# Another written order for the first eleven stretches of an attention kernel

## The chip, the cores and the metric

The kernel runs on one core of one Trainium2 chip. The metric is the device time of one execution in microseconds (us); lower is better. Five engines work side by side, each in the order of its own instruction stream: TensorE (PE; its weight loads are the row PEld), VectorE (DVE), ScalarE (ACT), GpSimd (POOL) and SyncE (SP), which here issues most of the DMAs. They meet by semaphores only.

## What is computed

From the reference, cut to what matters (bfloat16; S = Sq = 2048 rows, D = 640, 32 heads of 192, a window of W = 512 keys; w_gate, w_up: 640 x 1536):

```python
xn = _layernorm(A_x)
# attention without a mask, over the last 512 keys of the cache
q = (xn @ wq).reshape(B, Sq, Hq, Dh).transpose(0, 2, 1, 3)
scores = jnp.einsum("bhqd,bhkd->bhqk", q, k) * (Dh ** -0.5)
p = _softmax(scores, axis=-1)
s = jnp.einsum("bhqk,bhkd->bhqd", p, v) ... @ wo
# two rows of xn, those with the largest xn @ w_r, get a gated FFN's output added
b = _B_ref(xn, w_r, w_gate, w_up, w_down)
out = A_x + s * _silu(b)
```

## The kernel before

**Tiles.** The 2048 rows are 16 tiles of 128. A *step* i is one of (group g of four heads, block t5 of four tiles, pair pr of two heads), in that order; it has four *units*, one for each tile, n = 4 i + u. A unit is 128 rows by two heads. Units are put into *stretches*: S.0 and S.1 have two units each, all others three; there are 86 (0 to 85). All engines follow one written list of *tokens*: the function first (from L654 on) turns a token into instructions, and each engine gets its own in the order of the list. No scheduler changes that order (manual_schedule). The list of stretches 0 to 10 is the string FIRST; 11 to 84 are written by a function (stretch), and the last by another string.

**Tokens**, with unit n, head hh, step i:

- x.t5.lo.hi loads tiles lo to hi of block t5; k.p.hh, v.p, wq.p, wo.g.pr load keys, values and weights of a pair or group. An "a" at the end puts the load on ScalarE's queue instead of SP's.
- Statistics of a row tile: bn.n.c is half of one on VectorE (the second half also aggregates). as.n makes all of one tile's on ScalarE: two passes over 128x640 with a sum each (L235, L236), and a small step on GpSimd. sq, rc and pw make the reciprocal root: by ScalarE and VectorE, or by four GpSimd instructions for two or four tiles. sx and ex load tables of ScalarE's functions.
- ap.n.e writes the normalized tile xn on the engine e (v VectorE, a ScalarE, g GpSimd). turn.n.e turns it on TensorE and copies it out; xT.lo.hi turns two tiles by a DMA on SP. kt.q.e and kT.p do the same for keys. z.1 is one matmul on a tile of zeros, whose result nobody reads.
- q.i.c(.lo.hi) is one third (128 of the 384 columns) of a step's projection: five matmuls of 512 columns, or of 256 where lo.hi names half of the block. qe.i.c.e copies it, scaled, to SBUF.
- S.j: all scores of stretch j, two matmuls a head (contraction 128, L317, and 64, L324). M.n.hh: the negated row max (VectorE, L332). E.n.hh: exp with its row sum (ScalarE, L339). P.n: the unit's exps are turned by a DMA on SP (L344). O.n: eight matmuls with the values (L358). R.j: reciprocals of the sums. Oe.n.e: the output, divided, to SBUF. T.j(.lo.hi): its turning by a DMA on SP (L379). W.w: the product of one row tile with wo for a group, two times six matmuls of 320 columns (L406). We.w.e adds or copies it to the accumulator.
- B.j.slot runs background steps filed for that stretch. The earliest is filed for stretch 12, so every B in FIRST is empty.

**Buffers that order the work around the change.** Results of TensorE lie in two pools in PSUM, used in turn:

```python
    ps_f = pool("ps_f", 2, space=bass.MemoryType.PSUM)
    ps_p = pool("ps_p", 6, space=bass.MemoryType.PSUM)
```

From ps_f come turn, q, and an O without letter; from ps_p come scores (two a unit, so all six in a stretch of three units), W (two), kt, and an O with g. A matmul that opens a result waits until the one that had this buffer before is read: scores by E, q by qe, O by Oe, W by We. Exps have four buffers (freed when P has landed), pT and oT six, o_sb and x_in two: the load of block 2 waits for the ap of all four tiles of block 0, that of block 3 for block 1.

Of the kernel before, what the change touches and what calls it, by code (L numbers as in the profile page):

```python
# [21 lines left out]
def kernel(ctx, tc, A_x, A_k_cache, A_v_cache, A_wq, A_wo, B_x, B_w_r, B_w_gate, B_w_up, B_w_down, out):  # L22
    nc = tc.nc
    P = 128
    _, S, D = A_x.shape
# [3 lines left out]
    W = min(4096, max(256, Sk // 4))  # L29
# [412 lines left out]
    M = {}  # L442
# [347 lines left out]
    for j in range(2, NST):  # L790
        due = sum(st_of[4 * i] <= j + 1 for i, _ in todo)
        k = max(due, 2) if j % 4 != 1 else max(due, 3)
# [3 lines left out]
        k = 2 if len(ready) >= 2 and len(q_in[j]) <= 2 and (done + 1) <= 1.5 * (j - 4) else 1  # L796
        k = {NST - 4: 1, NST - 3: 1, NST - 2: 3, NST - 1: 2}.get(j, k)
# [69 lines left out]

    for token in FIRST:
# [43 lines left out]
```

## Time and profile before

| | us |
|---|---|
| median of 3 runs | 795.02 (794.94 to 795.55) |
| the profiled execution, its own time | 795.82 |
| its span, first to last instruction | 794.0 |
| TensorE busy | 783.4 |
| VectorE busy | 624.6 |
| ScalarE busy | 477.1 |
| GpSimd busy | 179.0 |

Times in views of the profile count from the span's start. A row of a timeline gives start, duration, engine, line, operation, output <- input, count, and in brackets the engine's idle time before it and who ended that. Consecutive instructions overlap at their ends, so the price of one in a series is the distance of starts. Section 2 of the page cuts the span in 40 slices and gives each engine's busy tenths; PEclk there is the clock granted to TensorE.

### The profile page before, as it was taken

To read this page: it belongs to the slowest core of one execution; us is meant where nothing else is said; L and a number is where in the kernel's file an instruction comes from. 1 tells how busy PE (TensorE), PEld (TensorE's weight loads), DVE (VectorE), ACT (ScalarE), POOL (GpSimd) and SP (SyncE) were. 2 spreads that over 40 slices of the span, in tenths; PEclk is the share of its full clock that TensorE was granted. 3 is DMA by queue.
4 is the path that set the end of the run, shared out by engine and by line. 5 is a ranking of instruction groups with operands and counts; after the bars stand their busy time and mean duration, and the time that the engine had idled before them with its cause. 6 is when DMAs were issued, how large, how long until landed. Compare 5 with 4: busy or idle time off the path is not lost. (4 is left out here: it accounts for less than half of the span.)

```text
span 794.0 us, 15678 instructions
## 1 busy us (share of the span) xinstructions
PE 783.4 (99%) x5758; PEld 481.9 (61%) x5759; DVE 624.6 (79%) x1247; ACT 477.1 (60%) x1285; POOL 179.0 (23%) x197
## 2 busy tenths in 40 slices
PE   8999999999999999999999999999999999999998
PEld 4456666656666566666566665666566666556666
DVE  7975677989787777777787777777788988777786
ACT  7856666557655656655566455566666865565651
POOL 3130000000010000000000599970000000165966
PEclk9999999999999999999999999999999999999999
DMA  9999998799989999799997999879998899998996
GB/s 255 194 198 204 197 212 152 138 179 192 194 134 207 201 192 218 136 220 192 202 217 150 170 170 199 169 136 179 200 159 149 134 192 190 184 195 151 181 163 141
DMA packets 453869, 143.80 MB, mean 181 GB/s; under 512 B 422446, under 2 KB 453424, under 8 KB 453792
## 3 DMA queue, kind: packets, MB, share of 16 engines
q1 hardware_dynamic: 452336, 140.39, 95.1%
q0 software_dynamic: 736, 1.84, 0.9%
q8 instruction: 45, 0.74, 0.4%
q10 hardware_dynamic: 720, 0.57, 0.3%
q14 instruction: 32, 0.26, 0.1%
HBM read 39.98 MB, written 2.62 MB: 54 GB/s over the span
## 5 line engine op out<-in xcount | busy, mean ns | idle before, releaser
L339 ACT ACTIVATE pexp<-sc,nm 128x512 bf16<-128x512 f32 x512 | 348.4, 697 | 266.0 <-issue 231.8
L332 DVE TENSOR_REDUCE nm<-sc 128x1 f32<-128x512 f32 x512 | 315.5, 683 | 77.1 <-PE sc L324 76.9
L303 PE MATMUL q_ps<-xnT,wq_p 128*128 128x512 bf16 (+1 forms) x980 | 225.9, 375 | 1.4 <-ACT o_sb L371 0.6
L406 PE MATMUL w_ps<-wo_g,oT 128*128 128x320 bf16 x1542 | 222.9, 298 | 0.0
L406 PEld LDWEIGHTS <-oT 128*128 128x128 bf16 x1542 | 150.3, 98 | 69.5
L358 PE MATMUL o_ps<-v_sb,pT 128*128 128x192 bf16 x2048 | 185.9, 246 | 2.3 <-DMA pT<-pexp 2.2
L358 PEld LDWEIGHTS <-pT 128*128 128x128 bf16 x2048 | 170.9, 98 | 18.6 <-DMA pT<-pexp 5.4
L373 DVE TENSOR_TENSOR o_sb<-o_ps,lsum 128x384 bf16<-128x384 f32 x244 | 134.6, 556 | 40.3 <-PE o_ps L358 22.2
L303 PEld LDWEIGHTS <-wq_p 128*128 128x128 bf16 x980 | 89.3, 98 | 124.4 <-issue 35.8
L317 PE MATMUL sc<-kT,qT 128*128 128x512 bf16 x512 | 125.2, 379 | 0.1
L420 DVE TENSOR_TENSOR s_acc<-s_acc,w_ps 128x320 f32<-128x320 f32 x192 | 92.6, 484 | 30.6 <-PE w_ps L406 30.6
L339 ACT ACTIVATION_READ_ACCUMULATOR pexp<-sc,nm 128x1 f32 x512 | 109.8, 215 | 0.0
L295 ACT ACTIVATE qT<-q_ps 128x512 bf16<-128x512 f32 (+1 forms) x179 | 99.3, 608 | 5.2 <-PE q_ps L303 5.1
L317 PEld LDWEIGHTS <-qT 128*128 128x128 bf16 x512 | 48.5, 98 | 41.8 <-issue 1.2
L324 PE MATMUL sc<-kT,qT 64*128 64x512 bf16 x512 | 70.2, 380 | 0.0
L324 PEld LDWEIGHTS <-qT 64*128 64x128 bf16 x512 | 18.0, 94 | 46.8 <-issue 35.8
L650 POOL TENSOR_TENSOR s_acc<-s_acc,xn 128x640 f32<-128x640 f32 x16 | 22.9, 1433 | 102.3 <-DVE s_acc L420 102.3
L629 POOL TENSOR_TENSOR xn<-xn,yh 128x640 bf16<-128x640 bf16 x32 | 44.6, 1394 | 2.7
L619 POOL DMA_DIRECT2D y_d<-y_sb x4 | 2.2, 551 | 181.2 <-DVE y_sb L616 181.2
L496 POOL DMA_DIRECT2D c_d<-cand x1 | 0.5, 544 | 163.7 <-DVE cand L494 163.7
L651 POOL TENSOR_TENSOR s_acc<-s_acc,x_fin 128x640 f32<-128x640 f32 x16 | 22.4, 1398 | 61.6 <-DVE lsum L348 54.5
L628 POOL TENSOR_SCALAR yh<-y_bc,oh 128x640 bf16<-128x640 bf16 x32 | 25.6, 799 | 6.0 <-DMA y_bc<-y_d 4.4
(109 smaller groups left out, 229.9 us busy)
## 6 DMA issues: line engine op xcount, KB each, us to landing
wq_p<-in_A_wq_dram SPq DMA_DIRECT2D x16, 480.0 KB, 4.7
wo_g<-in_A_wo_dram SPq DMA_DIRECT2D x16, 480.0 KB, 4.3
k_raw<-in_A_k_cache_dram SPq DMA_DIRECT2D x32, 192.0 KB, 3.4
v_sb<-in_A_v_cache_dram SPq DMA_DIRECT2D x16, 384.0 KB, 4.3
pT<-pexp SPq DMA_TRANSPOSE x256, 3.6
x_fin<-in_A_x_dram SPq DMA_DIRECT2D x16, 160.0 KB, 2.9
wgu<-in_B_w_gate_dram SPq DMA_DIRECT2D x15, 128.0 KB, 2.9
wgu<-in_B_w_up_dram SPq DMA_DIRECT2D x15, 128.0 KB, 3.7
```

Source lines behind the costliest of these rows:

```text
L295: nc.scalar.activation(out=out, in_=in_, func=ACT.Copy, scale=scale)
L303: nc.tensor.matmul(q_ps, lhsT=wq_of[g * PAIRS + pr][:, dc, c * P:(c + 1) * P], rhs=xnT[:, t5 * 4 + lo:t5 * 4 + hi, dc, :], start=(dc == 0) ...
L317: nc.tensor.matmul(sc_of[n][hh], lhsT=qT_of[i][:, 2 * hh, u * P:(u + 1) * P], rhs=kp[:, :, 2 * hh, :], start=True, stop=False)
L324: nc.tensor.matmul(sc_of[n][hh], lhsT=qT_of[i][hs, 1, u * P:(u + 1) * P], rhs=kp[hs, :, 1, :], start=False, stop=True)
L332: nc.vector.tensor_reduce(out=nm_of[j][:, c:c + 1], in_=sc_of[n][hh], axis=AX.X, op=ALU.max, negate=True)
L339: nc.scalar.activation(out=pe_of[n][:, hh, :], in_=sc_of[n][hh], func=ACT.Exp, bias=nm_of[j][:, c:c + 1], scale=1.0, accum_out=l_of[j][:, ...
L358: nc.tensor.matmul(ps[:, hh, :], lhsT=pT_of[n][:, hh, jj, :], rhs=v_sb[:, hh, jj, :], start=(jj == 0), stop=(jj == NJ - 1))
L373: nc.vector.tensor_tensor(out=osb_of[j][:, m], in0=ps, in1=l_of[j][:, 2 * m:2 * m + 2].unsqueeze(2).to_broadcast([P, 2, Dh]), op=ALU.mult)
L406: nc.tensor.matmul(w_ps, lhsT=oT_of[j][:, stretches[j].index(n), c % 3, :], rhs=wo_of[g][:, c, lo:hi], start=(c == 0), stop=(c == CPG - 1))
L420: nc.vector.tensor_tensor(out=acc, in0=acc, in1=w_ps, op=ALU.add)
L628: nc.gpsimd.tensor_scalar(out=yh, in0=M["y_bc"][:, j, :], scalar1=M["oh"][:, n, j:j + 1], scalar2=0.0, op0=ALU.mult, op1=ALU.add)
L629: nc.gpsimd.tensor_tensor(out=xn[:, n, :], in0=xn[:, n, :], in1=yh, op=ALU.add)
```

## The change

Only the string FIRST is different. Its tokens are the same up to these differences: which engine does a copy (the letters of Oe, qe, We, turn, kt), which O take their buffer from ps_p (g), which tiles' statistics are made by ScalarE (7, 4, 8, 10, 15 before; 5, 4, 11, 10, 12 after) and which projections are halved (q.2.0 before; q.1.2, q.2.1 and q.6.0 after); x loads are cut otherwise, the first now on SP; k.3.1 is on ScalarE's queue; T.9 is one DMA instead of two; there is one z.1 less, and all five z.1 come before the first turn. All else is the place in the list.

```diff
--- before.py
+++ after.py
@@ -851,18 +851,18 @@
 
     J0 = 11
     FIRST = """
-B.4.0 x.0.0.1.a x.0.1.3 z.1 bn.0.0 x.0.3.4 k.0.0 z.1 bn.1.0 bn.0.1 k.0.1 wq.0 sq.0.1 bn.1.1 z.1 rc.0.1 bn.2.0 z.1 sq.1.2 ap.0.v x.1.1.2 x.1.2.3 rc.1.2 bn.3.0 sx ex ap.1.v x.1.3.4 turn.0.a bn.2.1 bn.3.1 pw.2.4 turn.1.a kt.0.a x.1.0.1 kt.1.v B.5.2 z.1 q.0.2.0.2 qe.0.2.a.0.2 ap.2.g v.0 bn.5.0 ap.3.v B.3.1 q.0.0.0.2 bn.6.0 k.1.1 q.0.1.0.2 qe.0.1.v.0.2 qe.0.0.a.0.2 turn.3.v bn.6.1 z.1 as.7 k.1.0 turn.2.v bn.5.1 v.1 
-S.0 M.0.0 wq.1 q.0.0.2.4 M.0.1 q.0.2.2.4 as.4 qe.0.0.a.2.4 q.0.1.2.4 qe.0.2.v.2.4 pw.4.8 x.2.0.1 ap.4.g E.0.0 ap.7.g M.1.0 ap.5.v E.0.1 M.1.1 qe.0.1.a.2.4 x.2.1.3 x.2.3.4 E.1.0 
-S.1 q.1.2 kT.1 q.1.0 E.1.1 M.3.0 M.2.1 P.0 M.3.1 ap.6.g xT.4.6 M.2.0 E.3.0 P.1 qe.1.2.a qe.1.0.v E.3.1 q.1.1 O.0 E.2.0 E.2.1 bn.9.0 qe.1.1.v B.3.3 
-S.2 bn.11.0 O.1 R.0 xT.6.8 P.3 R.1 bn.11.1 Oe.0.v M.4.1 M.4.0 as.8 P.2 B.7.0 x.3.2.4 q.2.0.0.2 as.10 Oe.1.v qe.2.0.a.0.2 B.2.2 q.2.0.2.4 B.2.0 x.3.0.2 M.6.0 E.4.0 bn.9.1 E.6.0 q.2.2 E.4.1 M.5.0 T.0 E.5.0 qe.2.0.v.2.4 B.10.2 B.3.0 q.2.1 M.5.1 E.5.1 M.6.1 pw.8.12 qe.2.2.v E.6.1 ap.9.g qe.2.1.v B.5.3 ap.10.v bn.14.0 P.4 
-S.3 O.2 P.5 O.3 as.15 M.7.0 M.8.0 ap.8.g Oe.2.a M.9.1 Oe.3.v E.7.0 P.6 bn.13.0 xT.8.10 ap.11.v q.3.0 E.8.0 q.3.1 M.7.1 M.8.1 qe.3.0.a E.7.1 qe.3.1.v B.2.3 xT.10.12 q.3.2 E.8.1 O.4 M.9.0 P.7 O.5.g R.2 qe.3.2.a T.1 B.10.0 bn.13.1 Oe.4.v Oe.5.v B.4.1 E.9.0 E.9.1 P.9 bn.12.0 bn.12.1 
-S.4 O.6 M.10.0 M.12.0 M.10.1 q.4.1 P.8 wo.0.0 E.10.0 R.3 B.4.3 Oe.6.v O.7.g q.4.0 M.11.0 qe.4.1.v O.9 E.10.1 M.12.1 E.11.0 M.11.1 E.12.0 E.12.1 wo.0.1 O.8.g Oe.7.v Oe.8.v E.11.1 B.2.1 P.10 
-S.5 bn.14.1 qe.4.0.a Oe.9.a T.2.0.1 M.13.0 M.13.1 M.14.0 M.15.0 E.13.0 q.5.0 q.4.2 T.2.1.3 R.4 P.11 M.15.1 B.10.3 E.14.0 E.13.1 M.14.1 P.12 pw.12.16 ap.15.g O.10.g ap.14.g qe.5.0.v ap.13.g Oe.10.a qe.4.2.v W.0 E.15.0 We.0.v B.6.2 P.13 E.14.1 B.8.2 P.14 ap.12.g B.6.1 O.11.g xT.14.16 E.15.1 Oe.11.v B.7.1 O.12 Oe.12.v 
-S.6 q.5.1 q.5.2 M.17.0 M.16.0 M.16.1 qe.5.1.v E.16.0 M.18.1 E.17.0 E.16.1 R.5 W.1 M.17.1 T.3 qe.5.2.v E.17.1 M.18.0 We.1.v O.13 B.6.3 P.15 Oe.13.a xT.12.14 B.6.0 W.2 E.18.0 E.18.1 We.2.v T.4 O.14 v.2 O.15.g Oe.14.a Oe.15.a 
-S.7 q.6.0 qe.6.0.a P.16 M.21.0 R.6 M.19.0 M.20.1 q.6.2 P.17 E.19.0 M.19.1 M.20.0 E.19.1 E.20.0 q.6.1 E.21.0 O.16.g T.5 W.3 E.20.1 M.21.1 qe.6.2.a E.21.1 B.10.1 P.18 wq.2 W.4 We.4.a k.3.0 O.17 We.3.v P.19 qe.6.1.a Oe.16.v 
-S.8 M.23.1 P.21 O.18 P.20 Oe.17.a Oe.18.a k.2.0 q.7.1 qe.7.1.a R.7 q.7.0 M.22.0 E.22.0 M.22.1 M.24.1 B.5.0 O.19 k.2.1 E.22.1 Oe.19.v M.23.0 wq.3 E.23.0 B.7.3 M.24.0 B.5.1 W.5 P.22 qe.7.0.a We.5.a E.23.1 E.24.0 O.20 W.6 B.8.0 T.6 B.3.2 O.21 E.24.1 B.9.1 Oe.21.a We.6.v B.4.2 B.9.3 Oe.20.a 
-S.9 M.25.0 M.26.0 M.25.1 q.7.2 P.23 M.27.0 q.8.0 E.25.0 O.22.g M.26.1 qe.7.2.v E.25.1 R.8 E.26.0 E.26.1 k.3.1 O.23.g P.24 W.7 M.27.1 P.25 E.27.0 B.9.0 q.8.1 B.8.3 Oe.22.v P.26 qe.8.0.v We.7.v E.27.1 qe.8.1.a Oe.23.v 
-S.10 M.28.0 M.28.1 O.24 M.30.0 E.28.0 P.27 q.8.2 Oe.24.v B.7.2 E.28.1 E.30.0 M.30.1 R.9 qe.8.2.v kT.2 T.7 B.8.1 O.27.g M.29.0 T.8 E.29.0 O.25.g E.30.1 O.26.g q.9.0 M.29.1 E.29.1 kT.3 Oe.25.v W.8 Oe.26.a Oe.27.a P.28 wo.1.0 P.30 We.8.v W.9 We.9.a P.29 wo.1.1 v.3 qe.9.0.v T.9.0.2 T.9.2.3 B.9.2
+x.0.0.2 z.1 B.7.2 bn.0.0 x.0.3.4 bn.0.1 sx z.1 bn.1.0 B.4.0 z.1 z.1 k.0.0 x.0.2.3 bn.1.1 sq.0.1 z.1 rc.0.1 k.0.1 sq.1.2 bn.3.0 rc.1.2 ap.0.v ap.1.v ex wq.0 turn.0.a kt.0.a bn.2.0 bn.2.1 x.1.3.4 bn.3.1 turn.1.v B.2.0 kt.1.a q.0.2.0.2 qe.0.2.v.0.2 x.1.1.3 x.1.0.1 pw.2.4 ap.2.v k.1.1 q.0.1.0.2 ap.3.g k.1.0 qe.0.1.a.0.2 q.0.0.0.2 bn.7.0 qe.0.0.v.0.2 bn.7.1 v.1 turn.2.v wq.1 turn.3.v v.0 
+S.0 as.5 bn.6.0 q.0.0.2.4 M.0.0 as.4 q.0.2.2.4 E.0.0 M.0.1 qe.0.0.a.2.4 bn.6.1 pw.4.8 M.1.0 q.0.1.2.4 ap.4.g E.0.1 x.2.0.2 x.2.2.4 M.1.1 qe.0.2.a.2.4 qe.0.1.v.2.4 ap.5.v 
+S.1 E.1.0 bn.8.0 ap.7.v M.2.0 E.1.1 ap.6.v B.5.2 as.11 kT.1 M.3.0 P.0 E.2.0 q.1.0 M.2.1 q.1.1 qe.1.0.a B.4.2 qe.1.1.a bn.8.1 q.1.2.2.4 B.2.2 M.3.1 P.1 qe.1.2.v.2.4 E.3.0 q.1.2.0.2 E.2.1 E.3.1 B.2.3 B.5.3 O.0.g R.0 qe.1.2.v.0.2 bn.9.0 B.3.3 Oe.0.v xT.4.6 bn.9.1 xT.6.8 as.10 
+S.2 pw.8.12 M.4.0 M.5.0 R.1 M.4.1 P.2 E.4.0 O.1 Oe.1.a M.6.0 q.2.0 E.5.0 P.3 M.5.1 E.4.1 qe.2.0.a E.5.1 M.6.1 E.6.0 q.2.2 O.2.g qe.2.2.v Oe.2.v E.6.1 q.2.1.0.2 ap.10.v x.3.2.4 qe.2.1.v.0.2 B.4.1 q.2.1.2.4 bn.15.0 B.7.0 
+S.3 B.9.2 bn.15.1 R.2 x.3.0.2 ap.11.g ap.9.a O.3 qe.2.1.a.2.4 T.0 q.3.2 B.3.0 bn.13.0 M.7.0 ap.8.g P.4 M.8.0 M.9.0 Oe.3.a M.7.1 qe.3.2.v E.7.0 q.3.0 E.7.1 bn.14.0 E.8.0 O.4.g P.5 B.8.1 qe.3.0.a M.8.1 E.9.0 bn.14.1 xT.8.10 M.9.1 q.3.1 E.8.1 P.6 xT.10.12 P.7 P.8 E.9.1 O.5 Oe.4.v R.3 P.9 T.1 qe.3.1.v 
+S.4 M.10.0 O.6 Oe.5.a M.10.1 q.4.0 M.11.0 wo.0.0 E.10.0 B.10.1 Oe.6.v M.12.0 E.10.1 E.11.0 B.10.2 qe.4.0.a E.12.0 O.7.g M.12.1 wo.0.1 M.11.1 q.4.1 bn.13.1 O.8.g T.2.0.1 E.12.1 B.9.1 B.8.3 E.11.1 O.9 P.10 qe.4.1.v Oe.7.v Oe.8.a Oe.9.v P.11 
+S.5 as.12 B.6.1 M.13.0 T.2.1.3 E.13.0 q.4.2 M.13.1 M.14.0 pw.12.16 M.14.1 qe.4.2.a q.5.0 P.12 ap.15.v M.15.1 E.13.1 E.14.0 E.14.1 qe.5.0.v B.2.1 M.15.0 E.15.0 E.15.1 R.4 W.0 T.3 O.10 ap.14.g B.9.3 O.11 We.0.v 
+S.6 Oe.10.a Oe.11.v M.16.0 q.5.2 M.16.1 P.14 O.12 ap.12.a E.16.0 E.16.1 R.5 W.2 M.18.0 qe.5.2.a q.5.1 P.13 We.2.a ap.13.v xT.14.16 Oe.12.a M.17.1 xT.12.14 M.17.0 E.17.0 B.8.2 P.15 E.17.1 M.18.1 W.1 P.16 P.17 O.14 E.18.0 B.9.0 E.18.1 k.2.0 qe.5.1.v We.1.v O.13 Oe.13.a Oe.14.v 
+S.7 M.19.1 k.3.1.a O.15 T.4 Oe.15.v q.6.2 M.19.0 qe.6.2.a E.19.0 P.18 q.7.0 M.20.0 qe.7.0.v B.7.3 M.21.1 M.21.0 E.20.0 q.6.1 qe.6.1.a O.17.g T.5 R.6 E.19.1 O.16 M.20.1 E.20.1 q.6.0.0.2 B.5.0 B.10.0 B.4.3 W.3 E.21.0 qe.6.0.a.0.2 O.18.g We.3.v Oe.16.a E.21.1 P.19 Oe.17.a Oe.18.v B.7.1 R.7 W.4 B.8.0 We.4.a 
+S.8 q.7.1 M.22.0 E.22.0 M.22.1 q.6.0.2.4 E.22.1 B.3.2 M.24.0 M.23.0 P.20 E.23.0 P.21 O.19.g E.24.0 v.2 M.23.1 wq.2 E.23.1 qe.7.1.a M.24.1 W.5 qe.6.0.v.2.4 k.2.1 O.20 T.6 W.6 B.6.0 Oe.19.a We.6.v E.24.1 q.7.2 R.8 O.21.g We.5.v Oe.21.a 
+S.9 Oe.20.v qe.7.2.a q.8.1 q.8.0 P.23 M.25.0 E.25.0 M.26.1 P.24 M.25.1 M.27.0 M.26.0 P.22 wq.3 qe.8.0.v wo.1.0 B.3.1 M.27.1 qe.8.1.a E.25.1 E.26.0 O.23 E.27.0 E.26.1 O.22.g k.3.0 T.7 B.6.2 W.7 We.7.v Oe.22.a O.24 E.27.1 Oe.23.v 
+S.10 M.28.0 M.29.0 q.9.0 P.25 M.28.1 P.27 Oe.24.a M.29.1 E.28.0 M.30.1 E.28.1 q.8.2 P.26 B.6.3 R.9 qe.9.0.a E.29.0 W.9 E.29.1 M.30.0 kT.2 O.25.g We.9.v T.8 qe.8.2.v E.30.0 Oe.25.v W.8 kT.3 B.10.3 P.29 P.28 E.30.1 O.26.g O.27.g P.30 B.5.1 wo.1.1 Oe.26.v We.8.a v.3 Oe.27.v T.9
     """.split()
 
     for token in FIRST:
```

## The prediction

> **What bounds the kernel now.** I read the page's engine shares first, then the timeline of TensorE, and only then, for the stretches where TensorE stops, the timelines of the others.
>
> ```profile
> span 794.0 us, 15678 instructions
> PE 783.4 (99%) x5758; PEld 481.9 (61%) x5759; DVE 624.6 (79%) x1247; ACT 477.1 (60%) x1285; POOL 179.0 (23%) x197
> PEclk9999999999999999999999999999999999999999
> 104.00:790.00 686.00, 685.78 (x5082) 425.35 (x5080) 545.76 (x1077) 402.97 (x1088) 159.76 (x149) 1.00 0.95 177
> 20.00:40.00 20.00, 18.32 (x126) 9.77 (x125) 18.67 (x43) 16.58 (x45) 3.93 (x9) 1.00 1.15 197
> ```
>
> The last two rows are stretches of time: length, then busy time of PE, PEld, DVE, ACT, POOL. From 104 to 790 us TensorE is idle for 0.2 of 686 us, and that part of the program isn't changed. So the whole effect is the moment at which S.11 starts. Between 20 and 40 us TensorE stands still for 1.7 us and VectorE for only 1.3: there the softmax, not the matmuls, sets the pace. Starts of the stretches, and the waits, in TensorE's timeline (start, duration, [idle before <- who ended it]):
>
> ```profile
> 12.10 1.03 PE L317 MATMUL sc<-kT,qT 128*128 128x512 bf16 x4
> 17.09 3.41 PE L303 MATMUL q_ps<-xnT,wq_p 128*128 128x512 bf16 x15
> 21.17 0.83 PE L358 MATMUL o_ps<-v_sb,pT 128*128 128x192 bf16 x8 [0.67 <-DMA pT<-pexp]
> 21.84 1.46 PE L317 MATMUL sc<-kT,qT 128*128 128x512 bf16 x6
> 23.98 0.83 PE L358 MATMUL o_ps<-v_sb,pT 128*128 128x192 bf16 x8
> 28.67 1.56 PE L317 MATMUL sc<-kT,qT 128*128 128x512 bf16 x6
> 32.97 3.40 PE L303 MATMUL q_ps<-xnT,wq_p 128*128 128x512 bf16 x15 [0.57 <-ACT o_sb L371]
> 37.53 1.46 PE L317 MATMUL sc<-kT,qT 128*128 128x512 bf16 x6
> 44.07 0.83 PE L358 MATMUL o_ps<-v_sb,pT 128*128 128x192 bf16 x8 [0.52 <-DMA pT<-pexp]
> 45.32 0.83 PE L358 MATMUL o_ps<-v_sb,pT 128*128 128x192 bf16 x8 [0.41 <-DMA pT<-pexp]
> 45.99 1.46 PE L317 MATMUL sc<-kT,qT 128*128 128x512 bf16 x6
> 54.30 0.83 PE L358 MATMUL o_ps<-v_sb,pT 128*128 128x192 bf16 x8 [0.58 <-DMA pT<-pexp]
> 54.97 1.46 PE L317 MATMUL sc<-kT,qT 128*128 128x512 bf16 x6
> 64.60 1.68 PE L317 MATMUL sc<-kT,qT 128*128 128x512 bf16 x6
> 74.90 1.46 PE L317 MATMUL sc<-kT,qT 128*128 128x512 bf16 x6
> 77.04 0.83 PE L358 MATMUL o_ps<-v_sb,pT 128*128 128x192 bf16 x8
> 77.71 2.32 PE L303 MATMUL q_ps<-xnT,wq_p 128*128 128x512 bf16 x10
> 79.87 0.82 PE L358 MATMUL o_ps<-v_sb,pT 128*128 128x192 bf16 x8
> 80.53 1.79 PE L406 MATMUL w_ps<-wo_g,oT 128*128 128x320 bf16 x12
> 82.16 0.82 PE L358 MATMUL o_ps<-v_sb,pT 128*128 128x192 bf16 x8
> 103.67 1.46 PE L317 MATMUL sc<-kT,qT 128*128 128x512 bf16 x6
> ```
>
> The gapless run from 74.90 gives the price of each step, start to start: S 2.14, O 0.665, q (5 matmuls) 1.08, W 1.63 us. With them the work of S.3 is 8.05 us but it took 8.86; S.4 6.96 against 8.46; S.5 7.93 against 8.98; S.8 to S.10 28.8 against 28.8. In all some 5.8 us are lost between S.0 and S.11, nearly all before S.8. That is all an order could gain; what it could lose has no such end.
>
> **The change, part by part.** Most of it is permutation: the same tokens elsewhere. The count of statistics on ScalarE doesn't change (tiles 7, 4, 8, 10, 15 before; 5, 4, 11, 10, 12 after), and the B tokens in these stretches are empty. I follow the new order by hand: an instruction starts when the one before it on its engine is done and its inputs and a free buffer are there. Prices besides TensorE's:
>
> ```profile
> 4.47 0.89 DVE L165 BATCH_NORM_STATS2 stats<-x_in 128x6 f32<-128x320 bf16 x2 [0.18 <-DMA x_in<-in_A_x_dram]
> 6.54 0.43 DVE L253 TENSOR_SCALAR xn<-x_in,mv,rstd 128x640 bf16<-128x640 bf16 x1
> 9.43 1.88 PE L303 MATMUL q_ps<-xnT,wq_p 128*128 128x256 bf16 x15 [0.26 <-ACT xnT L261]
> 10.99 0.73 ACT L235 ACTIVATE junk_a<-x_in 128x640 bf16<-128x640 bf16 x1
> 12.80 0.74 ACT L235 ACTIVATE junk_a<-x_in 128x640 bf16<-128x640 bf16 x1
> 14.49 0.36 ACT L295 ACTIVATE qT<-q_ps 128x256 bf16<-128x256 f32 x1
> 14.75 0.68 ACT L339 ACTIVATE pexp<-sc,nm 128x512 bf16<-128x512 f32 x1
> 15.41 0.68 ACT L339 ACTIVATE pexp<-sc,nm 128x512 bf16<-128x512 f32 x1
> 25.34 1.63 PEld L303 LDWEIGHTS <-wq_p 128*128 128x128 bf16 x11 [0.26 <-DMA xnT<-xn]
> 26.09 1.12 SPq L101 DMA_DIRECT2D x_in<-in_A_x_dram  x2
> 30.52 0.74 ACT L235 ACTIVATE junk_a<-x_in 128x640 bf16<-128x640 bf16 x1 [0.72 <-DMA x_in<-in_A_x_dram]
> 30.87 1.87 DVE L332 TENSOR_REDUCE nm<-sc 128x1 f32<-128x512 f32 x3
> pT<-pexp SPq DMA_TRANSPOSE x256, 3.6
> ```
>
> So: one "as" holds ScalarE 1.75 us (10.99 to 12.80 to 14.49), an E 0.66 (14.75 to 15.41), a half-width qe 0.26 to 0.36, an M 0.6; a pT is there 3.6 us after its issue; half of a q costs 0.57 us (1.88 less the 0.17 tail, over 3), so a split q costs 0.06 more than a whole one; behind S.0 three are split now (q.1.2, q.2.1, q.6.0) and one was (q.2.0): 0.12 us, in the steps below. The warm-up matmul that goes stood in idle time.
>
> *Start.* Tile 0 moves from its own small load on ScalarE's queue into a first load of two tiles on SP. Bounds: 3.79 us, when it was there before, to 4.47, when the two-tile load beside it was (the wait of 0.18 in its row ends there; the 3.79 is that row's 4.47 less the wait and the bn of 0.5 ahead of it). I take 4.0, near the lower end, because only the first of two loads has to arrive. Then four bn (0.43), two aggregates, a reciprocal and bn.3.0 bring ap.0 to 6.55 against 6.54, because the old order waited at 4.47. turn.1's copy goes to VectorE and both kt copies to ScalarE, about as long; q.0.2 starts at 9.4 as before, S.0 at 12.1. The path to S.0 keeps its length; at 4.47 it would be 0.4 longer. v.0 is now asked for last of the first loads, at about 9; O.0 needs it at 21.9.
> The Trainium skill (DMA: Bandwidth & Descriptors, "Issuing engines are not separate DMA queues") says that loads issued by several engines share the same DMA engines, so that a second issuer saves only issue time. By that the load moved to SP loses little; the rows agree no closer than the 0.68 us between the two bounds.
>
> *S.0, S.1: +0.6.* as.5 and as.4 hold ScalarE from 11.05 to 14.55. Before, qe.0.0.a came next (14.49); now E.0.0 does, so the q_ps buffer is free at 15.55, not 14.85, and the third half of q waits for it; qe.0.2.a, behind E.0.1, ends at 16.47 and S.1's second matmul waits for that. S.1 ends at 17.70 against 17.09.
>
> *S.1, S.2: +0.64 in all.* as.11 (17.70 to 19.45) now stands ahead of E.2.0 and qe.1.0.a, which ends at 20.7: TensorE, ready for q.1.2 at 19.86, waits 0.85, and the rest of q.1.2, O.0 and S.2 with it. That takes the place of the old wait of 0.67 for pT.0, which now lies behind it. S.2's scores end at 24.62 against 23.98.
>
> *S.2 to S.3: +0.07.* O.1, q.2.0 (0.15 of wait: it now needs the second xT at once, which landed at about 25.3), q.2.2, O.2, two halves: S.3 at 29.4. Before it was 28.67, without O.2 (0.665).
>
> *S.3: −0.73.* Before, Oe.2.a stood behind as.15, which waited 0.72 us for x; now that statistic is VectorE's. Every exp that frees a score buffer ends before its turn (E.9.0 and E.9.1 excepted, S.4). 7.4 us of work, S.4 at 36.8 instead of 37.53.
>
> *S.4: −1.94.* Before, T.1 was ahead of P.9 and P.8 in SP's queue, and O.9 and O.8 waited 0.52 and 0.41. Now P.7, P.8, P.9 go first, O.8 and O.9 come last: P.8 issued at 37.4 when E.8.1 ends, there at 41.0, used at 42.7; P.9 38.9, 42.5, used at 43.4. S.4's scores lose 0.3 to E.9.1. S.5 at 44.05 instead of 45.99.
>
> *S.5: −3.05.* O.12, which waited 0.58 for its pT, moves into S.6. W.0's buffers come from E.13.0 and E.13.1 0.5 to 1 us ahead of their use. No wait is left: S.6 at 51.25, against 54.97 less O.12's 0.665.
>
> *S.6 to S.10: 1.1 back.* We.2.a and Oe.12.a now stand on ScalarE ahead of E.17.0, and W.1 needs that score's buffer: 0.85 lost in S.6, with O.14, O.13 and S.7's scores queued behind it (S.7 at 61.65, −2.3). S.7 regains the 0.3 it lost before (−2.6). In S.8, O.20 waits 0.55 for qe.7.1.a behind E.23.0, E.24.0 and E.23.1 (−2.0). S.9 and S.10 fit without a wait. k.3.1's issue, now on ScalarE's queue in S.7, falls where that engine has no exp ready. S.11 at 101.7 instead of 103.67: −1.95.
>
> *Allowance.* By hand no transfer is ever late. Four are within 0.4 us of it: xT for q.2.0, the load of x tiles 12 to 15 for bn.15.0, xT for q.4.0, pT.9. A wait of the old order for a pT was 0.4 to 0.67 us; one of these should come: +0.5. Sum: −1.45. The profiled execution of 795.82 us (its span 794.0) would be 794.4; the median of the runs shown, 795.02, lies 0.8 lower: **793.6 us**.
>
> **The rivals.**
> *Slower: ScalarE becomes the bound.* At the prices above it has about 20 us of work in S.0 to S.2, against 16.7 before: one statistic more (as.7 stood ahead of S.0), three full qe for one, and Oe.1. If its queue runs w later than I have it, P.2 and P.3 are later by w on SP, and with them the x load behind them. I have that load issued at 25.5 and there at 29.9, by the old order's 26.09 and 30.5, and bn.15.0 ready for it at 29.8. VectorE, not ScalarE, now stops for it, with M.7.0 and every later max queued behind; busy 18.67 of 20 us there, it can't catch up. So w passes whole to S.4: 793.6 + w. From w = 1.45 the gain is gone, from 3.0 it is slower by 0.2%; I take 3.2: **796.8**. For it: the saturated row and four buffers that TensorE waits for ScalarE to free. Against: ScalarE stood still 3.4 of those 20 us. 20%.
> *Gain given back.* The waits in S.6 and S.8 show that buffers freed by ScalarE limit TensorE once transposes don't. Two more such waits, of 0.7 each, leave no change: 795.0. For it: ScalarE's order has an Oe.a or We.a ahead of an E in every one of S.6 to S.10. Against: S.8 to S.10 ran gapless before with the same kind of order. 20%.
> *More gained.* No late transfer, and W.1's wait absent because E.17.0 comes earlier than I have it: −2.8, 792.2. For it: I took 0.60 to 0.65 for each M, and the row of three gives 0.62 with its tail. 18%.
> *Clock.* All five warm-up matmuls now stand before the first transpose, so the idle time ahead of q.0.2, by my times 8.25 to 9.43, isn't filled any more. How a slow clock looks:
>
> ```profile
> 1.19 3.81 PE L140 MATMUL warm_ps<-idle 128*128 128x512 bf16 x10 [1.19 <-DVE idle L137]
> ```
>
> Ten took 0.38 us each here against 0.216 later. If TensorE ran so once more for the same 3.8 us, it would do 1.6 us less: 795.2. Against: the PEclk row is at 9 throughout, the old start with its idle time included. 6%.
> The Trainium skill (TensorE: Matmul & The Clock Gate, Part 1) states a drop to half the clock after an idle window of about 3.4 us; by that rule gaps of 1.2 us cost nothing, and the PEclk row agrees as far as it goes.
> That the order does nothing can't be: the stretch with the waits is rewritten.
>
> **How the numbers follow.** The forecast, −1.45 with −2.7 to −0.5 as its own range, has 36%. A difference of 0.2%, 1.6 us, is about what a measurement of this kernel tells from no change. Faster by more: half of the forecast's share, 0.18, and the case of −2.8, 0.18. Within: the other half, the gain given back and the clock, 0.18 + 0.20 + 0.06 = 0.44. Slower by more: 0.20. The range leaves out the far halves of the two outer cases, 0.09 and 0.10: 792.2 to 796.8.
>
> **What would show it.** S.0 within 0.5 of 12.1; q.1.2 waiting for ScalarE's qT; S.4 near 36.8, S.6 near 51; no wait for pT in S.3 to S.5; waits in S.6 (W.1) and S.8 (O.20); S.11 at 101 to 103. I am wrong if S.4 starts after 38, if VectorE shows a wait for x of over 1 us, or if the granted clock dips.

## The result, and the profile after

The new order takes 792.87 us (median of 13 runs, 792.08 to 793.83) and the old one 794.98 beside it (13 runs, 793.84 to 795.83): a ratio of 0.9973, 95% interval 0.9964 to 0.9982, or 2.1 us less. The prediction was 793.6 in a range of 792.2 to 796.8. The profiled execution of the new kernel took 792.9 us, span 791.1; that of the old one lay 0.8 above its median, so the 2.9 us between the spans overstate the difference.

The page of the new kernel, the rows that answer to those shown of before:

```profile
span 791.1 us, 15694 instructions
PE 781.4 (99%) x5768; PEld 483.3 (61%) x5768; DVE 624.1 (79%) x1248; ACT 480.3 (61%) x1292; POOL 175.2 (22%) x192
PEclk9999999999999999999999999999999999999999
```

Same work, same clock. (TensorE's busy time is 2.0 us lower all the same. One reason: a matmul counts as busy to its modelled end, 0.83 us for an O whose price is 0.665, and where a wait follows, that end isn't covered by the next matmul; the new order has fewer waits.) The table by stretches of time (length, then busy time of PE, PEld, DVE, ACT, POOL) says where TensorE still stops behind S.0: up to S.3, and nowhere from S.3 to S.11 (from S.6 to S.11, not in the table, it is busy for 48.96 of 48.96 us).

```profile
12.33:30.53 18.20, 15.95 (x110) 8.79 (x108) 17.31 (x40) 17.59 (x48) 6.42 (x14) 1.00 1.23 241
30.53:37.91 7.38, 7.38 (x54) 4.17 (x52) 7.31 (x18) 5.72 (x16) 0.00 (x0) 1.00 1.12 213
37.91:44.86 6.95, 6.95 (x57) 4.33 (x55) 6.04 (x13) 5.89 (x18) 0.00 (x0) 1.00 1.09 150
44.86:52.18 7.32, 7.32 (x53) 4.19 (x51) 6.58 (x14) 6.79 (x20) 4.24 (x13) 1.00 1.07 260
```

TensorE's timeline after, the waits and the starts of the stretches (start, duration, [idle before <- who ended it]):

```profile
9.60 1.94 PE L303 MATMUL q_ps<-xnT,wq_p 128*128 128x256 bf16 x15 [1.21 <-DMA wq_p<-in_A_wq_dram]
...
15.76 0.70 PE L303 MATMUL q_ps<-xnT,wq_p 128*128 128x256 bf16 x5 [0.67 <-ACT qT L295]
...
21.29 1.25 PE L303 MATMUL q_ps<-xnT,wq_p 128*128 128x256 bf16 x10 [0.96 <-ACT qT L295]
...
23.04 1.46 PE L317 MATMUL sc<-kT,qT 128*128 128x512 bf16 x6
...
26.61 2.33 PE L303 MATMUL q_ps<-xnT,wq_p 128*128 128x512 bf16 x10 [0.60 <-DMA xnT<-xn]
...
30.53 1.46 PE L317 MATMUL sc<-kT,qT 128*128 128x512 bf16 x6
...
37.91 1.46 PE L317 MATMUL sc<-kT,qT 128*128 128x512 bf16 x6
...
44.86 1.52 PE L317 MATMUL sc<-kT,qT 128*128 128x512 bf16 x6
...
52.18 1.46 PE L317 MATMUL sc<-kT,qT 128*128 128x512 bf16 x6
...
58.78 1.79 PE L406 MATMUL w_ps<-wo_g,oT 128*128 128x320 bf16 x12
...
73.57 1.46 PE L317 MATMUL sc<-kT,qT 128*128 128x512 bf16 x6
...
79.64 0.82 PE L358 MATMUL o_ps<-v_sb,pT 128*128 128x192 bf16 x8
```

S.11 starts at 101.14 instead of 103.67. O.2 was moved ahead of S.3 and O.12 behind the start of S.6; with 0.665 for each, the new order stands against the old like this (us; minus is earlier, at equal work):

| at | forecast by hand | measured |
|---|---|---|
| S.0 | 0.0 | +0.23 |
| S.3 | +0.07 | +1.20 |
| S.6 | −3.06 | −2.13 |
| S.11 | −1.95, with the allowance −1.45 | −2.53 |

So in these two profiles the gain is made between S.3 and S.6 (3.3 us), a third of it is paid ahead of S.3, and nothing is given back afterwards. That 2.53 is more than the 2.1 of the medians fits the old kernel's profiled execution, which was a long one.

### The profile page after: what moved, and what is told of

It reads as the page before. It is cut to its first block, busy times and chain, and to the rows that moved or that the text cites. A ratio compares the mean times of both kernels' runs of the same rounds, so it can differ in the third digit from the quotient of the medians.

```text
span 791.1 us, 15694 instructions
## 1 busy us (share of the span) xinstructions
PE 781.4 (99%) x5768; PEld 483.3 (61%) x5768; DVE 624.1 (79%) x1248; ACT 480.3 (61%) x1292; POOL 175.2 (22%) x192
## 4 chain that ended last, share of the span: by engine, by line
PE 84%; DVE 0%; ACT 0%; issue 0%
PE w_ps L406 24%; PE q_ps L303 23%; PE o_ps L358 19%; PE sc L317 12%; PE sc L324 7%; DVE nm L332 0%; ACT pexp L339 0%; PE gu_ps L576 0%; PE y_ps L613 0%; DVE fin_o L433 0%; DVE w_ps L431 0%; PE tp_o L391 0%; ACT qT L295 0%
## 5 line engine op out<-in xcount | busy, mean ns | idle before, releaser
L295 ACT ACTIVATE qT<-q_ps 128x512 bf16<-128x512 f32 (+1 forms) x182 | 101.0, 607 | 4.6 <-PE q_ps L303 4.4
```

What stands on the lines that cost most here:

```text
L295: nc.scalar.activation(out=out, in_=in_, func=ACT.Copy, scale=scale)
```

## The experiments

All medians have a run of the old order beside them (794.66, 794.76 and 794.66 us in the three groups: e1 to e4, e5 to e8, e9 to e12). S.3, S.6 and S.11 are from each kernel's one profile. The executions of the old order beside them took 793.13 to 796.31 us, so some tenths between two profiles are no difference by themselves. O.12 stands ahead of S.6 in before, e2, e3, e4, e7, e9, behind its start in the others.

| | S.3 | S.6 | S.11 | median, us | ratio to before |
|---|---|---|---|---|---|
| before | 28.67 | 54.97 | 103.67 | 794.98 | 1 |
| after | 30.53 | 52.18 | 101.14 | 792.87 | 0.9973 |
| e1 old start, new S.3 to S.10 | 28.18 | 52.90 | 102.35 | 794.37 | 0.9994 (0.9985 to 1.0003) |
| e2 new start, old S.3 to S.10 | 30.41 | 54.59 | 102.94 | 794.42 | 0.9995 (0.9986 to 1.0004) |
| e3 old, T.1 later | 28.96 | 55.00 | 103.30 | 795.09 | 1.0005 (0.9996 to 1.0014) |
| e4 old, tile 15 on VectorE | 29.53 | 55.21 | 103.58 | 794.61 | 0.9998 (0.9989 to 1.0007) |
| e5 old, O.12 into S.6 | 29.24 | 53.29 | 103.14 | 795.12 | 1.0005 (0.9996 to 1.0015) |
| e6 old, O.12 and T.1 | 28.53 | 53.12 | 102.98 | 795.21 | 1.0009 (1.0000 to 1.0019) |
| e7 new, O.12 back | 30.44 | 54.96 | 103.40 | 796.05 | 1.0018 (1.0005 to 1.0031) |
| e8 new, copies ahead of exps | 31.06 | 53.12 | 102.09 | 793.29 | 0.9982 (0.9972 to 0.9991) |
| e9 as e7, P.12 first | 30.62 | 56.74 | 106.49 | 797.48 | 1.0036 (1.0022 to 1.0050) |
| e10 new, T.1 back | 30.36 | 52.59 | 101.55 | 793.05 | 0.9983 (0.9974 to 0.9992) |
| e11 new, one load on ScalarE | 35.05 | 56.70 | 105.83 | 798.35 | 1.0055 (1.0042 to 1.0067) |
| e12 e11 and halved q.2.0 | 37.25 | 58.89 | 108.24 | 799.21 | 1.0061 (1.0048 to 1.0074) |

**e1 and e2: the two halves of the change.** O.2 and bn.15.0 go with the half that needs them.

```diff
# e1: start, S.0, S.1, S.2 of the old order; S.3 to S.10 of the new one
+S.3 O.2 Oe.2.v ... bn.15.0 bn.15.1 ...
# e2: start, S.0, S.1, S.2 of the new order; S.3 to S.10 of the old one
+S.3 x.3.0.2 T.0 P.4 ap.9.g qe.2.1.a.2.4 bn.14.0 ... bn.15.1 ...
```

> Stretches 0 to 2 in the old order, 3 to 10 in the new one (O.2, Oe.2 and bn.15.0 come at the start of S.3; T.0, P.4, bn.14.0, the load of tiles 12 and 13 and tile 9 are done before). Theory: the gain is made in S.3 to S.5, where O no longer waits for a turned P, and the new S.0 to S.2 only cost (S.3 about 1.2 us later at equal work). Then S.3 starts at 28.7, S.4 near 36.8 and S.11 near 100: about 1 us faster than the new order, 791.8. Rival: the new early order sets the later one up (one O more done, statistics earlier); then waits for pT come back in S.3 to S.5 and the time is 794 to 795.

> Stretches 0 to 2 in the new order, 3 to 10 in the old one (O.2 and the first half of tile 15's statistics are done already, so as.15 becomes bn.15.1; what the old order had done by then comes at the start of S.3). Theory: S.3 at 30.5 and the old waits for pT in S.4 and S.5 again, less the 0.57 us behind as.15: S.11 near 104.3, time 795.6, no faster than the old order. Rival (the early order sets the gain up): no waits for pT, S.11 near 101.5, 793.

Neither half alone is told from no change (0.3 and 0.2 us); both together make 2.1. In e1 the old start brings TensorE to S.3 1.7 us earlier at equal work (28.18 plus O.2's 0.665, against 30.53), and there it waits for the softmax; S.4 starts at 38.35, later than in after (37.91). TensorE's timeline of e1:

```profile
34.75 0.82 PE L358 MATMUL o_ps<-v_sb,pT 128*128 128x192 bf16 x8 [0.54 <-ACT pexp L339]
36.33 1.24 PE L303 MATMUL q_ps<-xnT,wq_p 128*128 128x512 bf16 x5 [0.76 <-DVE qT L293]
```

In e2 the old S.3 to S.6 waits for pT again, 0.29 us ahead of O.8 and 0.32 ahead of O.12, less than in the old order:

```profile
53.92 0.84 PE L358 MATMUL o_ps<-v_sb,pT 128*128 128x192 bf16 x8 [0.32 <-DMA pT<-pexp]
```

In e1 a head start ahead of S.3 was worth nothing, since the softmax was not as far; the slow start of the new order is therefore not simply a loss that could be taken off again. And e1 has O.12 late, as the new order has, so that place alone doesn't make the gain either.

**e3: T.1 behind P.9 and P.8 in the old order, nothing else.**

```diff
-S.3 ... qe.3.2.a T.1 B.10.0 bn.13.1 ... P.9 bn.12.0 bn.12.1
-S.4 ... q.4.1 P.8 wo.0.0 ...
+S.3 ... qe.3.2.a B.10.0 bn.13.1 ... P.9 bn.12.0 bn.12.1
+S.4 ... q.4.1 P.8 T.1 wo.0.0 ...
```

> The old order with one token moved: T.1 behind P.9 and P.8 in SP's queue. Theory: P.9 and P.8 are issued 1.3 us earlier, O.9 and O.8 no longer wait (0.52 and 0.41 us), S.5 at 45.1 instead of 45.99: 794.1 if nothing later takes the place. Rival: P.9 and P.8 are late because their exps are, or the next transposes come late instead: S.6 unchanged near 55, 795.0.

The waits at O.8 and O.9 go and S.5 starts 1.04 earlier (44.95 for 45.99), but S.6 starts at 55.00 as before (54.97): O.10 now waits, and O.12 still does. TensorE's timeline of e3:

```profile
50.51 0.83 PE L358 MATMUL o_ps<-v_sb,pT 128*128 128x192 bf16 x8 [0.82 <-DMA pT<-pexp]
...
54.33 0.83 PE L358 MATMUL o_ps<-v_sb,pT 128*128 128x192 bf16 x8 [0.48 <-DMA pT<-pexp]
```

**e4: the statistics of tile 15 on VectorE in the old order.** `as.15` becomes `bn.15.0 bn.15.1`.

> The old order with tile 15's statistics on VectorE (bn.15.0 bn.15.1) in the place where ScalarE made them. Theory: Oe.2.a no longer stands behind a wait for x, TensorE's 0.57 us at 32.97 goes and S.4 starts at 37.0: 794.5. Rival: VectorE, busy 93% there, gets 1.1 us more and every max comes later: S.4 at 37.5 or later, 795.0 to 796.

The wait for ScalarE's copy of O.2 becomes one of the same 0.57 us for VectorE's copy of O.3, and S.3 takes 9.57 instead of 8.86. TensorE's timeline of e4:

```profile
35.24 2.32 PE L303 MATMUL q_ps<-xnT,wq_p 128*128 128x512 bf16 x10 [0.57 <-DVE o_sb L373]
```

So moving that statistic off ScalarE does not by itself make S.3 shorter. That the other tokens around it had to make room on VectorE is argued; no run here takes them one by one.

**e5 and e6: O.12 into S.6 in the old order, alone and with e3's edit.**

```diff
-S.5 ... Oe.11.v B.7.1 O.12 Oe.12.v
-S.6 ... M.18.0 We.1.v O.13 ...
+S.5 ... Oe.11.v B.7.1
+S.6 ... M.18.0 We.1.v O.12 Oe.12.v O.13 ...
```

> The old order with O.12 and Oe.12 moved from the end of S.5 into S.6, behind W.1. Theory: S.5 could not end before P.12 had landed (about 54.2 us), whatever was saved ahead of it; with O.12 away S.6 starts at 53.7 instead of 55.0, 0.6 us earlier at equal work, and S.11 near 103.1: 794.4. Rival: the wait moves to another O in S.6 and nothing changes, 795.0.

> The old order with both moves, T.1 behind P.9 and P.8 and O.12 into S.6. If the two waits add up: S.5 at 45.0 and S.6 at 52.8, S.11 near 102.2, 793.5. If SP's queue is the limit and the wait only moves (O.10 waited 0.8 us with T.1 late): S.6 at 53.8 and S.11 near 103.1, 794.4, no better than O.12 alone.

O.12's wait is gone and S.6 starts a microsecond earlier at equal work, but takes 10.9 us for 10.2 of work, and S.11 gains only 0.5 to 0.7 in the profile, nothing in the medians. The exps have four buffers, and a buffer is free when its P has landed. ScalarE waited for that in the old order already, ahead of the third exp from the end of S.5, which started at 52.92; in e5 the same exp starts at 52.46. So the last exps of S.5 follow an earlier P in the same queue, S.6's scores need the buffers that these exps read, and with O.12 out of the way TensorE comes there too early (the row of the scores is 1.93 us long for 1.46). ScalarE's timeline, before and e5:

```profile
52.92 0.69 ACT L339 ACTIVATE pexp<-sc,nm 128x512 bf16<-128x512 f32 x1 [0.57 <-DMA pT<-pexp]
```

```profile
52.46 0.69 ACT L339 ACTIVATE pexp<-sc,nm 128x512 bf16<-128x512 f32 x1 [0.70 <-DMA pT<-pexp]
```

**e7: the new order with O.12 put back at the end of S.5.**

```diff
-S.5 ... O.11 We.0.v
-S.6 Oe.10.a Oe.11.v M.16.0 q.5.2 M.16.1 P.14 O.12 ap.12.a ... Oe.12.a ...
+S.5 ... O.11 We.0.v Oe.10.a O.12
+S.6 Oe.11.v M.16.0 q.5.2 M.16.1 P.14 ap.12.a ... Oe.12.a ...
```

> The new order with O.12 put back to the end of S.5, behind O.11 (with Oe.10 ahead of it). Theory: it waits for P.12, issued at 50.1 and there at about 53.5: 1.3 us lost, S.6 at 54.2, S.11 at 102.4 instead of 101.1, 794.1. Rival: the place of O.12 doesn't matter in the new order since P.12 comes early enough; S.6 at 52.9 and 792.9.

This step (Oe.10.a goes with O.12, which needs the buffer that it reads) takes back the whole gain: S.6 at 54.96, as in the old order to 0.01. The ten executions fall into two groups, and the median of 796.05 lies between them: five took 794.4 to 795.3 us at a granted clock of 1.000, among them the profiled one (794.98), and five took 796.8 to 797.7 at 0.998. The first group is where the old order beside it is (794.76). What the second lost besides goes with the clock: 0.2% of 797 us would be 1.6 us, an estimate, of the 2.1 between the groups. TensorE's and SP's rows of e7:

```profile
54.29 0.83 PE L358 MATMUL o_ps<-v_sb,pT 128*128 128x192 bf16 x8 [2.04 <-DMA pT<-pexp]
```

```profile
45.35 3.25 SPq L344 DMA_TRANSPOSE pT<-pexp  x2
48.70 1.24 SPq L379 DMA_TRANSPOSE oT<-o_sb  x1
50.02 1.26 SPq L344 DMA_TRANSPOSE pT<-pexp  x1
```

P.12 (50.02) could go out only when P.10, P.11 and the second T.2 had left SP, and its result was there 4.3 us later. In the five orders that ask for O.12 ahead of S.6 it starts at 54.30 (before), 53.92 (e2), 54.33 (e3), 54.54 (e4) and 54.29 (e7), though S.5 started anywhere from 44.77 to 46.29: how early TensorE comes to O.12 changes little. The old order issued P.12 at 50.9 and had its result 3.3 us later, e7 at 50.0 and 4.3 us later; why the second took longer, no run here shows. So the new order does not have P.12's result earlier; it asks for O.12 later.

**e8: in the new order, S.0's copies of q ahead of its exps, and as.11 behind two copies.**

```diff
-S.0 ... q.0.2.2.4 E.0.0 M.0.1 qe.0.0.a.2.4 ... ap.4.g E.0.1 ... qe.0.2.a.2.4 ...
-S.1 ... ap.6.v B.5.2 as.11 ... qe.1.1.a ...
+S.0 ... q.0.2.2.4 qe.0.0.a.2.4 E.0.0 M.0.1 ... ap.4.g qe.0.2.a.2.4 E.0.1 ...
+S.1 ... ap.6.v B.5.2 ... qe.1.1.a as.11 ...
```

> The new order with its two waits for ScalarE taken away: qe.0.0 and qe.0.2 ahead of E.0.0 and E.0.1, and as.11 behind qe.1.1. If ScalarE bounds the first three stretches: the waits of 0.67 and 0.96 us go, S.2 at 21.5 instead of 23.0, S.3 at 29.1 and S.11 near 99.7: 791.5. If SP's queue does: q.2.0 waits until xT lands at 26.6 all the same, S.3 at 30.3, S.11 near 101: 792.8.

TensorE's wait of 0.67 us at 15.76 goes, and S.1 and S.2 come 0.5 and 0.3 earlier; then TensorE waits between its scores, and S.3 is later than in after. TensorE's timeline of e8:

```profile
21.03 1.25 PE L303 MATMUL q_ps<-xnT,wq_p 128*128 128x256 bf16 x10 [0.72 <-ACT qT L295]
...
23.85 1.04 PE L317 MATMUL sc<-kT,qT 128*128 128x512 bf16 x3 [0.25 <-ACT pexp L339]
25.19 0.38 PE L317 MATMUL sc<-kT,qT 128*128 128x512 bf16 x1 [0.29 <-ACT pexp L339]
```

What the exps give up ahead comes back as waits for them. The medians of e8 and after (793.29 and 792.87) are not told apart.

**e9: e7 with P.12 ahead of the second T.2.**

```diff
-S.5 as.12 B.6.1 M.13.0 T.2.1.3 E.13.0 ... q.5.0 P.12 ap.15.v ...
+S.5 as.12 B.6.1 M.13.0 P.12 T.2.1.3 E.13.0 ... q.5.0 ap.15.v ...
```

> The order of e7 (O.12 back at the end of S.5), with P.12 asked for ahead of T.2.1.3. Theory (P.12 lands late because it stands behind others in SP's queue, which is never idle there): P.12 is issued at 48.8 instead of 50.0, its exps are there 1.25 us earlier, TensorE's idle time ahead of O.12 falls from 2.04 to about 0.8, S.6 starts at 53.7 instead of 54.96, and the time is 794.8 (e7: 796.0, after: 792.9). Rival (the landing hangs on the exp or on the traffic of the DMA engines, not on the place in the queue): S.6 again at 54.9, 796.0.

Both expectations were wrong: the time is 797.48, and S.6 starts at 56.74. P.12 went out at 49.0 and its result was there 3.3 us later, at 52.3 instead of 54.3, so its place in the queue was what held it, as the theory has it; but T.2.1.3, now behind it, frees o_sb (two buffers) so much later that Oe.10.a waits, and O.12 needs the buffer that Oe.10.a reads. ScalarE's and TensorE's timelines, then the stretches of time of e9:

```profile
54.97 0.73 ACT L371 ACTIVATE o_sb<-o_ps,lsum 128x192 bf16<-128x192 f32 x2 [2.04 <-DMA oT<-o_sb]
```

```profile
55.75 1.20 PE L358 MATMUL o_ps<-v_sb,pT 128*128 128x192 bf16 x8 [3.33 <-ACT o_sb L371]
56.74 2.77 PE L317 MATMUL sc<-kT,qT 128*128 128x512 bf16 x6
```

```profile
57.00:58.00 1.00, 1.00 (x3) 0.30 (x2) 0.00 (x0) 0.00 (x0) 0.00 (x0) 0.50 1.41 202
```

The 3.33 us of idle time cost once more: the granted clock (the column behind POOL) was 0.50 afterwards, and O.12 and the six score matmuls took 1.20 and 2.77 us for 0.83 and 1.46. One of the six executions kept its clock (1.000, the others 0.998) and took 795.34 us; whether it waited less is not on record.

**e10: the new order with T.1 ahead of P.8 and P.9, as it was before.**

```diff
-S.3 ... P.7 P.8 E.9.1 O.5 Oe.4.v R.3 P.9 T.1 qe.3.1.v
+S.3 ... P.7 T.1 P.8 E.9.1 O.5 Oe.4.v R.3 P.9 qe.3.1.v
```

> The new order, with T.1 ahead of P.8 and so of P.9, as the old order had it. Theory of the prediction's step for S.4 (T.1's 1.3 us of SP's queue is paid by O.8 and O.9): P.8 and P.9 are issued at 39.4 and 41.1, there at about 43.0 and 44.7, O.9 waits 0.4 to 0.6; S.5 at 45.3 instead of 44.86, S.6 at 52.7 instead of 52.18, 793.4. Rival (T.1's place is nothing by itself, as in e3; where the O stand is what counts): no wait, S.5 at 44.9, 792.9. Second rival (the wait comes and S.5's slack for other tokens takes it up): S.5 at 45.3, S.6 at 52.3, 793.0.

As the first theory has it, O.9 waits, and everything behind it is 0.41 later, S.5 (45.27 for 44.86), S.6 (52.59 for 52.18) and S.11 (101.55 for 101.14) alike; the medians, 793.05 and 792.87, don't tell the two kernels apart. TensorE's timeline of e10:

```profile
44.60 0.83 PE L358 MATMUL o_ps<-v_sb,pT 128*128 128x192 bf16 x8 [0.41 <-DMA pT<-pexp]
```

In the profiles T.1's place is worth 0.4 us in the new order and nothing at S.6 in the old one (e3), where O.12 stands behind it and takes what it gives.

**e11 and e12: a try at a better start.** e11 puts the load of tile 2 on ScalarE's queue, so that wq is asked for earlier; e12 also halves q.2.0.

```diff
-... k.0.0 x.0.2.3 bn.1.1 ...
+... k.0.0 x.0.2.3.a bn.1.1 ...
# e12, in S.2, besides
-q.2.0 ... qe.2.0.a
+q.2.0.0.2 q.2.0.2.4 ... qe.2.0.a.0.2 qe.2.0.a.2.4
```

> The new order, with the load of row tile 2 on ScalarE's queue instead of SP's, so that the first load of wq is asked for at about 3.1 instead of 3.72. Theory (SP's issue time set the landing of wq, 9.60, which TensorE waited for 1.21 us): q.0.2 at 9.0, S.0 at 11.8 instead of 12.33, and 0.5 us less at S.11 unless VectorE's turns take it up: 792.4. Rival (the bytes ahead of wq on the shared DMA engines set it): q.0.2 at 9.5 to 9.6, S.0 unchanged, 792.9.

> As e11, and the two q of S.2's first third are halved (q.2.0), its first half needing only the first turned pair of row tiles. Theory (TensorE's wait of 0.60 us for the second pair is a loss by itself): the wait is gone for a price of 0.06, S.3 at 29.5 to 30.0 instead of 30.53, with the 0.5 of e11 792.0. Rival (these stretches are set by ScalarE's and VectorE's work, as e8 says: what TensorE doesn't wait for here it waits for a little later): S.3 to S.4 as in e11, 792.4 to 792.9.

e11 was 5.5 us slower than after, since something else became late. wq was asked for at 3.14, as meant, and landed 5.2 us later, at 8.3 (in after 3.72, and 5.8 later, 9.5). That is earlier by more than the issue, but a load ahead of it had left the way too, so e11 does not tell theory and rival apart. The load of tile 2 left ScalarE only at 6.25. The trace puts the wait down to a landing of keys, and the program shows why: the loads and transposes of SP and ScalarE share eight semaphores in turn, and this load got the one of k.0.0, issued at 1.76 and landed 4.5 us later, and waits for it though it needs no keys. VectorE, in order, stood in bn.2.0 for the load until 11.27, with turn.1's copy behind, which q.0.2 needs. Timelines of ScalarE, VectorE and TensorE in e11:

```profile
6.25 0.40 ACTq L101 DMA_DIRECT2D x_in<-in_A_x_dram  x1
6.70 0.48 ACT L225 ACTIVATE rstd<-mv,eps_t 128x1 f32<-128x1 f32 x2 [4.47 <-DMA k_raw<-in_A_k_cache_dram]
```

```profile
11.27 0.89 DVE L165 BATCH_NORM_STATS2 stats<-x_in 128x6 f32<-128x320 bf16 x2 [2.92 <-DMA x_in<-in_A_x_dram]
...
12.91 0.44 DVE L261 COPY xnT<-tp 128x640 bf16<-128x640 bf16 x1
```

```profile
13.50 3.15 PE L303 MATMUL q_ps<-xnT,wq_p 128*128 128x256 bf16 x15 [4.04 <-DVE xnT L261]
...
17.44 1.03 PE L317 MATMUL sc<-kT,qT 128*128 128x512 bf16 x4
```

Here too the clock fell (15 matmuls in 3.15 us for 1.94). What the two show all the same: of the 5.11 us that S.0 came later in e11, 4.69 are still there at S.11. And e12's halved q.2.0 took away the wait for xnT and brought others of 0.47 and 0.91 for ScalarE's copies; S.2 to S.3 took 8.66 us instead of 7.43. No order that ran was faster than the new one; e8 and e10 are not told apart from it.

## Why the prediction was right, point by point

*What bounds the kernel.* Held: from 101.14 on TensorE stops as little as before, and the effect is the start of S.11.

*Start.* Tile 0's load cost nothing, as taken: the first bn started at 3.94 us. Missed: tile 2 got a load of its own ahead of it, and so wq was asked for at 3.72 instead of 3.14 and TensorE waited 1.21 for it; S.0 is 0.23 later. The prediction followed every x load and not the load behind them in SP's queue.

*S.0 to S.2.* The waits named were there, for the reasons named, with 0.67 and 0.96 us (0.85 forecast for the second). *S.2 to S.3:* the allowance for one late transfer was due here: q.2.0 waited 0.60 for the second xT, not 0.15. With 0.23 of the start and 0.3 of S.0 to S.2, and some 0.1 more, this makes S.3 1.1 later than forecast.

*S.3 to S.5.* −3.3 us measured, −3.1 forecast, and every wait of the old order gone: the steps for S.4 and S.5 were right in place and size. S.4 itself, later by the miss ahead of S.3, started at 37.91, just short of the 38 named as a sign of being wrong. Their reasons were right together and too simple apart. The forecast added up T.1's place, tile 15's statistic and O.12's place as if each were worth its wait. e3, e4, e5 and e6 show that in the old order each is worth nothing: the wait comes back at the next P in SP's queue, at the buffer that a P frees, or on VectorE. e10 and e7 show that in the new order T.1 is worth 0.4, in the profile, and O.12's place the whole gain; e9 shows that P.12's place in SP's queue says when its result is there; and e1, with O.12 late behind the old start, is not told from no change. Which tokens of the start and of S.0 to S.2 the gain needs stays open.

*S.6 to S.10, "1.1 back": the step that failed.* It took W.1 to need the buffers of E.17.0 and E.17.1, and O.20 that of q.7.1. Neither did:

```profile
58.84 0.70 ACT L339 ACTIVATE pexp<-sc,nm 128x512 bf16<-128x512 f32 x1
...
79.96 0.60 ACT L295 ACTIVATE qT<-q_ps 128x512 bf16<-128x512 f32 x1
```

These rows of ScalarE's timeline of the new kernel are E.17.0 and qe.7.1.a; W.1 began at 58.78 and O.20 at 79.64, ahead of both. In the built program W.1 has the two buffers of W.2, and O.20 that of the second half of q.6.0, all read earlier. The pools don't hand their buffers out by turns, as the description of the kernel put it; in both places the result got one whose reader stands ahead of it in the list. By what rule it is picked, no run here shows. Without those two waits S.6 to S.11 took 48.96 us instead of the 50.45 by hand.

*The rivals.* "ScalarE becomes the bound" had its place right in part (ahead of S.3, where 1.1 us more were lost than forecast, some by waits for ScalarE, some by wq and xT) and its price wrong: VectorE had no wait for x, and S.3 took 7.38 us of 7.38 of work. "Gain given back" didn't happen. "More gained" (792.2) is the nearest of the rivals, for the reason it gave, W.1's wait absent, but by the buffer and not by an earlier E.17.0. "Clock" didn't happen at 1.21 us of idle time; it did in e9 and e11, behind 3.33 and 4.04.

*Why the sum held.* Two misses of opposite sign, 1.1 us late ahead of S.3 (0.5 of it allowed for) and 1.5 us that weren't given back. That they nearly cancelled is luck; the part between S.3 and S.6, which makes the gain, was not. The forecast of 793.6 was 0.7 too slow.

## What to carry to other kernels

Where one queue issues transfers back to back, as SP did here, a consumer that waits for one gained little from work saved ahead of it: ask whether the consumer can be asked for later, and check what the transfer's landing frees besides. Follow all tokens of such a stretch together, because edits that were worth nothing one by one in the old order (T.1, O.12) are parts of a new order worth 2.1 us, and putting one O back took it all away. Read from the built program which buffer a result really gets, before a wait for it is put into a sum.

## What was not expected of the hardware

In e7's profiled execution 2.04 us of idle time cost TensorE no clock (the eight matmuls behind it took 0.83 as ever); in e9's, 3.33 us cost half of it (granted 0.50 from 57 to 58 us); in e11's, behind 4.04 us, fifteen matmuls took 3.15 us for 1.94. The Trainium skill (TensorE: Matmul & The Clock Gate, Part 1) gives an idle window of about 3.4 us; 3.33 here, from the modelled end of the last matmul, agrees with it.

One kernel can lose the clock in one execution and keep it in the next: five of e7's ten executions had a mean granted clock of 0.998 and took 2 us more than the five with 1.000, and one of e9's six kept 1.000. How long TensorE waited in the executions without a profile is not on record.

A DMA transpose of one unit's exps held SP for 1.24 to 1.91 us (P.10 to P.12 of e7), and its data was there 3.8 us after its issue (median of the new kernel's 256), 4.3 for P.12 of e7. With two P and one T ahead of it, P.12 went out 4.7 us after the first of them (45.35 to 50.02).

A load asked for on another engine's queue need not go out earlier: e11's left ScalarE at 6.25 us, behind the landing of keys whose semaphore it shares, where that engine's row shows 4.47 us of idle time.
